# Transposing q and k by DMA instead of on TensorE, in a fused attention and MLP-mixer kernel

## The chip, the cores and the metric

The kernel runs on one core of a Trainium2 chip. The metric is the device time of one execution in microseconds (us), and lower is better. A core has five engines that run side by side: TensorE (PE in the profile, with PEld for its weight loads), VectorE (DVE), ScalarE (ACT), GpSimd (POOL) and SyncE (SP), which here only issues DMAs. Sixteen DMA engines move the data.

## The reference

The reference is causal attention with a decay bias, followed by a mixer block (an MLP over the tokens, then an MLP over the channels). Shapes are 8 batches, 8 heads, 576 tokens and 64 channels per head.

```python
def _attn_ref(q, k, v, s):                     # q, k, v: (8, 8, 576, 64), s: (8, 8, 576)
    scores = (1 / np.sqrt(D)) * np.matmul(q, k.transpose(0, 1, 3, 2))
    cum = np.cumsum(np.maximum(s, 0.0), axis=-1)
    bias = -(cum[:, :, :, None] - cum[:, :, None, :])
    scores = np.where(causal, -1e9, scores + np.minimum(bias, 0.0))
    attn = np.exp(scores - np.max(scores, axis=-1, keepdims=True))
    attn = attn / (np.sum(attn, axis=-1, keepdims=True) + 1e-09)
    return np.matmul(attn, v)

def _moe_ref(x, w_tok1, w_tok2, w_ch1, w_ch2):  # x: (8, 576, 512)
    h = np.maximum(x.transpose(0, 2, 1) @ w_tok1, 0.0) @ w_tok2
    u = x + h.transpose(0, 2, 1)
    return u + np.maximum(u @ w_ch1, 0.0) @ w_ch2
```

q and k are drawn as 0.1 times a normal variable, so the products of q and k are tiny beside the bias. The comparison with the reference hardly notices a wrong q or k.

## The kernel before

The kernel is built by a small list scheduler in Python, called the planner here. Each operation is registered with the engines that may do it and a guessed cost for each; the planner simulates the machine with these guesses and so fixes which engine does what, and in which order. These are the cost functions and the part that loads and casts one pair of heads:

```python
def c_dve(n, two=False):                       # guessed us for n elements on VectorE
    occ = 0.07 + n * (0.00053 if two else 0.00104)
    return occ, occ + 0.22

def c_pool(n, per=0.0022):                     # on GpSimd
    occ = 0.10 + n * per
    return occ, occ + 0.25

def stage_qk(b, h):                            # batch b, heads h and h+1
    f, n = Buf(r_qf), Buf(r_qn)
    for i, src in enumerate((k, q)):
        # token number = p * R + r: partition p holds R = 6 neighbouring tokens, long pieces for the DMA
        nc.sync.dma_start(out=f.t[:, i, :, :, :].rearrange("p e r d -> p e (r d)"),
                          in_=src[b, h : h + 2, :, :].rearrange("e (p r) d -> p e (r d)", r=R))
        ...
        # cast to bf16, on GpSimd from the second batch on
        nc.gpsimd.tensor_copy(out=n.t[:, i, :, :, :], in_=f.t[:, i, :, :, :].rearrange("p e r d -> p r e d"))
    ...
```

Because each partition holds six neighbouring tokens, six transposes of 96 columns give the tokens in the order r, p. The copy that takes the result out of PSUM (TensorE's result memory) also puts them back in the order p, r. These transposes and evictions are what the change replaces. The scores, the exponentials and the mask multiplies follow:

```python
def pair(b, h):
    qT, kT, E = Buf(r_qT), Buf(r_kT), Buf(r_E)          # rings of three buffers each
    for ti, dst in ((0, kT), (1, qT)):
        pt = Buf(r_sc, False)                            # a PSUM bank
        def tr(ti=ti, pt=pt):
            o = pt.t[:, :].bitcast(BF16)
            for r in range(R):
                nc.tensor.transpose(out=o[:, r * PR : (r + 1) * PR],
                                    in_=nat.t[:, ti, r, :, :].rearrange("p e d -> p (e d)"), identity=ident[0:PR, 0:PR])
        P.op({"PE": (R * 0.045, R * 0.045 + 0.3, tr)}, ...)
        def un(p0, p1, pt=pt):
            return pt.t[p0:p1, :].bitcast(BF16)[:, 0 : R * PR].rearrange("d (r p) -> d p r", r=R)
        ...
        # k: one copy of 128 partitions; q: two copies of 64 partitions, one per head; on ScalarE or VectorE
        nc.vector.tensor_copy(out=kT.t[:, 0:S].rearrange("d (p r) -> d p r", r=R), in_=un(0, 128))
    ...
            nc.tensor.matmul(out=o[:, :, c0 : c0 + e - a], lhsT=kT.t[:, j0 : j0 + 128],
                             rhs=qT.t[:, :, a:e], start=True, stop=True)          # scores
    ...
            nc.scalar.activation(out=E.t[:, :, EB[pc] : EB[pc] + 256], in_=..., func=AF.Exp, scale=0.125)
    ...
                    nc.vector.tensor_tensor(                                      # the mask multiply
                        out=E.t[:, :, d0 : d0 + n], in0=E.t[:, :, d0 : d0 + n],
                        in1=keep[:, k0 : k0 + n].unsqueeze(1).to_broadcast([128, 2, n]), op=ALU.mult)
    ...
                        nc.tensor.matmul(out=o[:, ic, 0 : D + 1], lhsT=E.t[:, hh, d0 : d0 + 128],
                                         rhs=vp.t[:, jc, h + hh, 0 : D + 1], ...)  # attention times v
```

The mask multiply has two inputs, both in SBUF (the on-chip memory of all tiles outside the PSUM banks). GpSimd's own work before the change is the cast of q and k and the scaling of v. The mixer of the third batch on already uses DMA transposes for its own activations, so the change extends a technique that the kernel has.

## Time and profile before

| | before |
|---|---|
| median of 3 runs (lowest to highest) | 330.56 us (329.26 to 331.84) |
| span of the profiled run, mean granted TensorE clock | 330.5 us, 0.982 of full speed |
| TensorE idle in the span | 330.5 - 308.9 = 21.6 us |

The page's first part gives, for each engine, the busy time, the share of the span and the number of instructions:

```profile
PE 308.9 (93%) x2424; PEld 178.6 (54%) x2457; DVE 207.2 (63%) x511; ACT 207.4 (63%) x367; POOL 101.1 (31%) x137
```

TensorE is busy nearly all the time. (It has 2,457 weight loads but 2,424 matmuls on record, so some 33 matmul records are missing.) The chain of waits, followed back from the last instruction, says the same:

```profile
PE 75%; DVE 14%; ACT 3%; DMA 3%; issue 2%; SPq 1%; POOL 0%; ACTq 0%
```

The table of stretches of the kernel before has the stretch, its length, then busy time with number of instructions for TensorE, its weight loads, VectorE, ScalarE and GpSimd, then the granted clock, the DMA share and GB/s:

```profile
75.00:130.00 55.00, 53.18 (x469) 32.03 (x472) 40.36 (x101) 38.75 (x68) 20.57 (x25) 1.00 0.78 173
130.00:250.00 120.00, 118.86 (x959) 69.07 (x969) 81.20 (x204) 85.50 (x149) 38.97 (x49) 1.00 0.62 149
```

From 75 to 250 us TensorE idles only 3 us at full clock. What it waits for is little and scattered. The view of TensorE's waits (engine, tile and line, what it waited for, then total, times and longest) holds these lines, in a list sorted by total:

```profile
PE psc_112 L657 <- ACT E_86 L663: 2.1, 1, 2.1
...
PE pav_115 L689 <- DVE E_84 L671: 0.5, 2, 0.3
```

The second line is attention times v waiting for a mask multiply: 0.5 us in the whole run. The next lines, from the groups of instructions, are the mask multiplies on three buffers, a cast on GpSimd, and two of the evictions that the change removes. The columns are line, engine, operation, out<-in, shapes, count, then busy us and mean ns of one, then idle time before them and what ended it:

```profile
L671 DVE TENSOR_TENSOR E_84<-E_84,keep 128x256 bf16<-128x256 bf16 (+1 forms) x55 | 17.2, 343 | 11.1 <-ACT E_84 L663 10.6
L671 DVE TENSOR_TENSOR E_85<-E_85,keep 128x256 bf16<-128x256 bf16 (+1 forms) x55 | 16.7, 331 | 8.9 <-ACT E_85 L663 8.7
L671 DVE TENSOR_TENSOR E_86<-E_86,keep 128x256 bf16<-128x256 bf16 (+1 forms) x50 | 14.8, 323 | 10.3 <-ACT E_86 L663 10.1
L575 POOL CAST qkn_76<-qkf_73 96x768 bf16<-96x768 f32 x22 | 18.3, 853 | 37.2 <-issue 18.2
L641 DVE COPY qT_78<-psc_113 64x576 bf16<-64x576 bf16 x7 | 5.3, 756 | 1.2 <-ACT qT_78 L639 0.6 <-PE psc_113 L619 0.4
L639 ACT COPY qT_79<-psc_113 64x576 bf16<-64x576 bf16 x7 | 4.4, 633 | 3.3 <-PE psc_113 L619 1.6 <-DVE qT_79 L641 1.6
```

The 160 mask multiplies take 17.2 + 16.7 + 14.8 = 48.7 us, with means of 323 to 343 ns; an eviction takes 0.76 us on VectorE or 0.63 us on ScalarE. In the timeline of TensorE (start us, duration, what), two groups of six transposes start 0.25 us apart, which is what one group costs:

```profile
129.58 0.42 PE L619 MATMUL psc_114<-ident,qkn_75 96*128 96x96 bf16 x6
129.83 0.42 PE L619 MATMUL psc_112<-ident,qkn_75 96*128 96x96 bf16 x6
```

### The profile page before, as it was taken

Reading aid. Unit: us, or ns where it says so; the run is one execution under the profiler, and the core shown is the slowest. Engines: PE = TensorE matmul, PEld = TensorE weight load, DVE = VectorE, ACT = ScalarE, POOL = GpSimd, SP = SyncE. Lnnn points to the kernel's source line nnn. Section 1 sums busy time; section 2 is a strip of 40 time slices with the busy share of each in tenths; the row PEclk is TensorE's granted clock in tenths of the full one; section 3 lists DMA queues with packets and bytes.
Section 4 is the critical chain, followed back from the end, with each engine's and each line's share of the span. In section 5 each row is a group of like instructions: output and inputs, shape, how many; then the busy total and the mean of one; then the engine's idle time right before and its main releaser. Section 6 shows DMA issues by size and latency. Waiting matters only on the chain.

```text
span 330.5 us, 6536 instructions
## 1 busy us (share of the span) xinstructions
PE 308.9 (93%) x2424; PEld 178.6 (54%) x2457; DVE 207.2 (63%) x511; ACT 207.4 (63%) x367; POOL 101.1 (31%) x137
## 2 busy tenths in 40 slices
PE   6888899979899999999999999999999799999992
PEld 2455486646665555555774554556764355446640
DVE  7698963789965756576776566576786454450021
ACT  4675777388886367974885278766889457406600
POOL 5455429757518022450146011821110000000000
PEclk9699999999999999999999999999999989999998
DMA  7999999999982549636944649266459710042031
GB/s 194 212 271 350 387 228 248 244 285 225 244 179 74 127 155 223 148 84 196 196 94 119 155 158 221 76 110 219 121 138 204 217 70 0 1 129 81 3 98 69
DMA packets 77272, 54.14 MB, mean 164 GB/s; under 512 B 54320, under 2 KB 70256, under 8 KB 77232
## 3 DMA queue, kind: packets, MB, share of 16 engines
q1 hardware_dynamic: 77232, 53.64, 65.7%
q8 instruction: 21, 0.34, 0.5%
q14 instruction: 19, 0.16, 0.2%
HBM read 40.65 MB, written 9.44 MB: 152 GB/s over the span
## 4 chain that ended last, share of the span: by engine, by line
PE 75%; DVE 14%; ACT 3%; DMA 3%; issue 2%; SPq 1%; POOL 0%; ACTq 0%
PE pmx_118 L883 12%; PE pmx_119 L865 9%; PE pmx_118 L865 8%; PE pmx_117 L865 8%; PE pmx_117 L883 7%; PE pmx_119 L883 7%; PE psc_112 L657 3%; PE pav_115 L689 2%; PE psc_113 L657 2%; PE psc_114 L657 2%; PE pav_116 L689 2%; DMA qkf_73<-in_k_dram 2%; PE pmx_117 L791 2%; PE pmx_117 L812 2%; DVE E_86 L671 2%
## 5 line engine op out<-in xcount | busy, mean ns | idle before, releaser
L865 PEld LDWEIGHTS <-wc_70 128*128 128x128 bf16 x624 | 59.2, 98 | 30.7 <-issue 0.5
L883 PEld LDWEIGHTS <-gb_107 128*128 128x128 bf16 x240 | 22.8, 99 | 25.6 <-issue 1.3
L575 POOL CAST qkn_75<-qkf_72 96x768 bf16<-96x768 f32 x19 | 17.1, 923 | 43.2 <-issue 12.9
L575 POOL CAST qkn_76<-qkf_73 96x768 bf16<-96x768 f32 x22 | 18.3, 853 | 37.2 <-issue 18.2
L883 PE MATMUL pmx_118<-wc_71,gb_107 128*128 128x512 bf16 x116 | 28.9, 393 | 0.2
L883 PEld LDWEIGHTS <-ga_106 128*128 128x128 bf16 x192 | 18.0, 98 | 19.6
L575 POOL CAST qkn_77<-qkf_74 96x768 bf16<-96x768 f32 x19 | 15.7, 843 | 30.7 <-ACT gb_107 L872 10.3
L671 DVE TENSOR_TENSOR E_84<-E_84,keep 128x256 bf16<-128x256 bf16 (+1 forms) x55 | 17.2, 343 | 11.1 <-ACT E_84 L663 10.6
L865 PE MATMUL pmx_118<-uTb_105,wc_70 128*128 128x320 bf16 x128 | 22.6, 299 | 0.1
L865 PE MATMUL pmx_119<-uTb_105,wc_70 128*128 128x320 bf16 x128 | 22.6, 299 | 0.0
L865 PE MATMUL pmx_117<-uTb_105,wc_70 128*128 128x320 bf16 x128 | 22.6, 299 | 0.0
L671 DVE TENSOR_TENSOR E_85<-E_85,keep 128x256 bf16<-128x256 bf16 (+1 forms) x55 | 16.7, 331 | 8.9 <-ACT E_85 L663 8.7
L548 POOL TENSOR_TENSOR vp_90<-vf_88,wT 128x512 bf16<-128x512 f32 (+1 forms) x20 | 20.6, 1053 | 2.2 <-DMA vf_88<-in_v_dram 1.9
L671 DVE TENSOR_TENSOR E_86<-E_86,keep 128x256 bf16<-128x256 bf16 (+1 forms) x50 | 14.8, 323 | 10.3 <-ACT E_86 L663 10.1
L872 ACT ACTIVATE gb_107<-pmx_119 128x320 bf16<-128x320 f32 x23 | 10.2, 442 | 17.4 <-PE pmx_119 L865 16.0
L548 POOL TENSOR_TENSOR vp_89<-vf_87,wT 128x512 bf16<-128x512 f32 (+1 forms) x15 | 15.4, 1041 | 6.0 <-PE pav_116 L689 4.7
L865 PE MATMUL pmx_118<-uTa_104,wc_70 128*128 128x512 bf16 (+1 forms) x79 | 17.1, 336 | 0.1
L865 PE MATMUL pmx_119<-uTa_104,wc_70 128*128 128x512 bf16 (+1 forms) x80 | 17.1, 336 | 0.0
L883 PE MATMUL pmx_117<-wc_71,ga_106 128*128 128x512 bf16 x69 | 16.9, 379 | 0.2
L865 PE MATMUL pmx_117<-uTa_104,wc_70 128*128 128x512 bf16 (+1 forms) x77 | 16.6, 335 | 0.2
L970 PE MATMUL pmx_117<-zero 128*128 128x512 bf16 (+6 forms) x44 | 14.2, 418 | 1.5 <-DVE zero L425 1.2
L883 PE MATMUL pmx_118<-wc_71,ga_106 128*128 128x512 bf16 x57 | 14.3, 379 | 0.2
(284 smaller groups left out, 695.9 us busy)
## 6 DMA issues: line engine op xcount, KB each, us to landing
vf_87<-in_v_dram SPq DMA_DIRECT2D x16, 256.0 KB, 6.6
vf_88<-in_v_dram SPq DMA_DIRECT2D x16, 256.0 KB, 5.5
qkf_74<-in_k_dram SPq DMA_DIRECT2D x14, 288.0 KB, 4.1
qkf_74<-in_q_dram SPq DMA_DIRECT2D x14, 288.0 KB, 4.4
qkf_72<-in_k_dram SPq DMA_DIRECT2D x13, 288.0 KB, 3.8
qkf_72<-in_q_dram SPq DMA_DIRECT2D x13, 288.0 KB, 4.4
qkf_73<-in_k_dram SPq DMA_DIRECT2D x13, 288.0 KB, 4.8
qkf_73<-in_q_dram SPq DMA_DIRECT2D x13, 288.0 KB, 5.2
```

The source lines that it names most:

```text
L548: eng.tensor_tensor(out=vp.t[p0 : p0 + n, c, :, 0:D], in0=vf.t[p0 : p0 + n, c, :, :], in1=wT[p0 : p0 + n, cw, b * H : b * H + H].unsqueeze ...
L575: nc.gpsimd.tensor_copy(out=o, in_=a)
L657: nc.tensor.matmul(out=o[:, :, c0 : c0 + e - a], lhsT=kT.t[:, j0 : j0 + 128], rhs=qT.t[:, :, a:e], start=True, stop=True)
L671: nc.vector.tensor_tensor(out=E.t[:, :, d0 : d0 + n], in0=E.t[:, :, d0 : d0 + n], in1=keep[:, k0 : k0 + n].unsqueeze(1).to_broadcast([128, ...
L689: nc.tensor.matmul(out=o[:, ic, 0 : D + 1], lhsT=E.t[:, hh, d0 : d0 + 128], rhs=vp.t[:, jc, h + hh, 0 : D + 1], start=(jc == j_lo), stop=( ...
L791: nc.tensor.matmul(out=pm.t[:, ha * D : hb * D], lhsT=w1[:, NJ if odd and c == NJ - 1 else c, t * 128 : t * 128 + 128], rhs=x.t[:, c, ha * ...
L812: nc.tensor.matmul(out=pm.t[:, :], lhsT=w2[:, t, w0 : w0 + 128], rhs=h1.t[:, t, :], start=(t == 0), stop=(t == NTC - 1))
L865: nc.tensor.matmul(out=pm.t[:, 0 : e - a], lhsT=wc1[:, m, cc * 128 : cc * 128 + 128], rhs=uT.t[:, m, a:e], start=(m == 0), stop=(m == NMC ...
L872: lambda cc=cc, pm=pm, a=a, e=e: nc.scalar.activation(out=g.t[:, cc, a:e], in_=pm.t[:, 0 : e - a], func=AF.Relu),
L883: nc.tensor.matmul(out=pm.t[:, :], lhsT=g.t[:, cc, c * 128 : c * 128 + 128], rhs=wc2[:, cc, :], start=(cc == 0), stop=(cc == NCC - 1))
L970: f.fn = lambda t=r.tiles[slots[0]], n=n: nc.tensor.matmul(out=t[:, 0:n], lhsT=zero[:, 0:128], rhs=zero[:, 0:n], start=True, stop=True)
```

## The change

The intent is to relieve TensorE, which bounds the kernel. For batches 2 to 7 (24 of the 32 head pairs) SyncE issues two DMA transposes per pair, from the cast tile into a new ring of three tiles named tr. The tokens come out in the order r, p, so three reordering copies per pair, on GpSimd or VectorE, write kT and qT. To make room a tile of ones shrank to one broadcast column, which doesn't bear on the argument.

```diff
+    r_tr = ring("tr", 3, [128, 2, R, PR], BF16)
...
+        if b >= 2:
+            raw = Buf(r_tr)
+            for ti in range(2):
+                def trd(ti=ti):
+                    nc.sync.dma_start_transpose(out=raw.t[:, ti, :, :],
+                                                in_=nat.t[:, ti, :, :, :].rearrange("p r e d -> p (r e d)"))
+                P.op({"SP": (0.6, 0, trd)}, reads=[(nat, ti)], writes=[(raw, ti)], prio=0, dma=0.85)
+            for (p0, p1, ti, dst, key) in ((0, 128, 0, kT, (kT, 0)), (0, 64, 1, qT, (qT, 0)), (64, 128, 1, qT, (qT, 1))):
+                def cp(eng, p0=p0, p1=p1, ti=ti, dst=dst):
+                    o = dst.t[p0:p1, 0:S] if dst is kT else dst.t[p0:p1, p0 // 64, :]
+                    o = o.rearrange("d (p r) -> d p r", r=R)
+                    i = raw.t[p0:p1, ti, :, :].rearrange("d r p -> d p r")
+                    eng.tensor_copy(out=o, in_=i)
+                P.op({"POOL": (*c_pool(576, 0.0011), lambda cp=cp: cp(nc.gpsimd)),
+                      "DVE": (*c_dve(576), lambda cp=cp: cp(nc.vector))}, reads=[(raw, ti)], writes=[key],
+                     prio=b * 10 + h - 1)
+        else:
             (the TensorE transposes and the PSUM evictions, as before)
```

The planner is told that a copy takes 0.10 + 576 x 0.0011 = 0.73 us on GpSimd and that a DMA transpose holds SyncE for 0.6 us.

More of the change, by code (lines that the diff above doesn't have):

```diff
@@ L456 @@
     s_sb = sb("s_sb", [64, S], FP32, fast)
-    one_sb = sb("one_sb", [64, S], FP32, fast)
+    ones = sb("ones", [128, 1], FP32, fast)
+    one_sb = ones[0:64, 0:1].to_broadcast([64, S])
     cum = sb("cum", [64, S], FP32)
@@ L462 @@
     nc.sync.dma_start(out=s_sb[:, :], in_=s.rearrange("b h s -> (b h) s"))
-    nc.vector.memset(one_sb[:, :], 1.0)
+    nc.vector.memset(ones[:, :], 1.0)
     nc.vector.memset(wn[:, S:640], 0.0)
@@ L475 @@
     P.op({"DVE": (1.3, 1.6, lambda: nc.vector.tensor_tensor_scan(
-        out=cum[:, :], data0=one_sb[:, :], data1=s_sb[:, :], initial=0.0, op0=ALU.mult, op1=ALU.add))},
+        out=cum[:, :], data0=one_sb, data1=s_sb[:, :], initial=0.0, op0=ALU.mult, op1=ALU.add))},
         reads=["sr"], writes=["cum"], prio=-1)
@@ L505 @@
     bad = sb("bad", [128, 4 + NSQ], FP32, fast)
-    ones = sb("ones", [128, 1], FP32, fast)
     flagf = sb("flagf", [1, 1], FP32, fast)
@@ L509 @@
     nc.vector.memset(bad[:, :], 0.0)
-    nc.vector.memset(ones[:, :], 1.0)
     P.op({"DVE": (1.3, 1.6, lambda: nc.vector.tensor_tensor_scan(
-        out=pre[:, :], data0=one_sb[:, :], data1=wn[:, 0:S], initial=0.0, op0=ALU.mult, op1=ALU.add))},
+        out=pre[:, :], data0=one_sb, data1=wn[:, 0:S], initial=0.0, op0=ALU.mult, op1=ALU.add))},
         reads=["wn"], writes=["pre"], prio=50)
@@ L612, in pair @@
         odd = b % 2
-        for ti, dst in ((0, kT), (1, qT)):
-            pt = Buf(r_sc, False)
-            def tr(ti=ti, pt=pt):
-                o = pt.t[:, :].bitcast(BF16)
-                for r in range(R):
-                    nc.tensor.transpose(out=o[:, r * PR : (r + 1) * PR],
-                                        in_=nat.t[:, ti, r, :, :].rearrange("p e d -> p (e d)"), identity=ident[0:PR, 0:PR])
-            P.op({"PE": (R * 0.045, R * 0.045 + 0.3, tr)}, reads=[(nat, ti)] + pads, writes=[(pt, 0)], holds=[dst], prio=(np_, 2))
-            def un(p0, p1, pt=pt):
-                return pt.t[p0:p1, :].bitcast(BF16)[:, 0 : R * PR].rearrange("d (r p) -> d p r", r=R)
-            if dst is kT:
-                def evk(eng, un=un):
-                    o = kT.t[:, 0:S].rearrange("d (p r) -> d p r", r=R)
-                    if eng == 0:
-                        nc.scalar.copy(out=o, in_=un(0, 128))
-                    else:
-                        nc.vector.tensor_copy(out=o, in_=un(0, 128))
-                P.op({"ACT": (*c_act(576), lambda evk=evk: evk(0)), "DVE": (*c_dve(576), lambda evk=evk: evk(1))},
-                     reads=[(pt, 0)], writes=[(kT, 0)], prio=1)
-            else:
-                for hh in range(2):
-                    def evq(eng, hh=hh, un=un):
-                        o = qT.t[hh * 64 : hh * 64 + 64, hh, :].rearrange("d (p r) -> d p r", r=R)
@@ new lines, in pair, with tr, un, evk @@
+        if b >= 2:
[15 more added lines that the diff above has]
+        else:
+            for ti, dst in ((0, kT), (1, qT)):
+                pt = Buf(r_sc, False)
+                def tr(ti=ti, pt=pt):
+                    o = pt.t[:, :].bitcast(BF16)
+                    for r in range(R):
+                        nc.tensor.transpose(out=o[:, r * PR : (r + 1) * PR],
+                                            in_=nat.t[:, ti, r, :, :].rearrange("p e d -> p (e d)"), identity=ident[0:PR, 0:PR])
+                P.op({"PE": (R * 0.045, R * 0.045 + 0.3, tr)}, reads=[(nat, ti)] + pads, writes=[(pt, 0)], holds=[dst], prio=(np_, 2))
+                def un(p0, p1, pt=pt):
+                    return pt.t[p0:p1, :].bitcast(BF16)[:, 0 : R * PR].rearrange("d (r p) -> d p r", r=R)
+                if dst is kT:
+                    def evk(eng, un=un):
+                        o = kT.t[:, 0:S].rearrange("d (p r) -> d p r", r=R)
@@ L638, in evq @@
                         if eng == 0:
-                            nc.scalar.copy(out=o, in_=un(hh * 64, hh * 64 + 64))
+                            nc.scalar.copy(out=o, in_=un(0, 128))
                         else:
-                            nc.vector.tensor_copy(out=o, in_=un(hh * 64, hh * 64 + 64))
-                    P.op({"ACT": (*c_act(576), lambda evq=evq: evq(0)),
-                          "DVE": (*c_dve(576), lambda evq=evq: evq(1))},
-                         reads=[(pt, 0)], writes=[(qT, hh)], prio=1)
+                            nc.vector.tensor_copy(out=o, in_=un(0, 128))
@@ new lines, in pair, with evq @@
+                    P.op({"ACT": (*c_act(576), lambda evk=evk: evk(0)), "DVE": (*c_dve(576), lambda evk=evk: evk(1))},
+                         reads=[(pt, 0)], writes=[(kT, 0)], prio=1)
+                else:
+                    for hh in range(2):
+                        def evq(eng, hh=hh, un=un):
+                            o = qT.t[hh * 64 : hh * 64 + 64, hh, :].rearrange("d (p r) -> d p r", r=R)
+                            if eng == 0:
+                                nc.scalar.copy(out=o, in_=un(hh * 64, hh * 64 + 64))
+                            else:
+                                nc.vector.tensor_copy(out=o, in_=un(hh * 64, hh * 64 + 64))
+                        P.op({"ACT": (*c_act(576), lambda evq=evq: evq(0)),
+                              "DVE": (*c_dve(576), lambda evq=evq: evq(1))},
+                             reads=[(pt, 0)], writes=[(qT, hh)], prio=1)
```

## The prediction

> **What bounds the kernel now.** From about 100 to 250 us TensorE does: the table of stretches gives it 148.5 us busy in those 150 us (clock 1.00), while VectorE has 100, ScalarE 103, GpSimd 49 us and the DMA engines are 61% busy. The chain of waits agrees: 75% of the span is TensorE, mostly channel-MLP matmuls at 0.215 us per 512 columns, their full pace. VectorE's 14% of the chain lies mostly before 100 us.
>
> **What is removed.** For 24 of 32 head pairs, two groups of six 96-column transposes. In the timeline such a group holds TensorE 0.26 us (129.58 to 129.83), so 48 x 0.26 = 12.3 us of TensorE, nearly all in the saturated stretch. Also 72 PSUM evictions: ScalarE 0.63 us, VectorE 0.75 us each, about 50 us. Chain pieces "q evicted on VectorE, then ScalarE" (130.9, 202.3, 277.7 us) go.
>
> **What is added.**
> - 48 DMA transposes of 96x768 from SyncE's queue. The existing 128x512 ones take 1.2 us of issue, start 1.3 us apart, and land after 2.4 us. Scaled by bytes (1.125) to blocks (6 for 4) I estimate 1.4 to 1.8 us of issue and 2.6 to 3.5 us to landing. [...] some 217 GB/s within a burst, about 100 GB/s at the issue pace. So 67 to 86 us of SyncE's queue, and 0.8 us of all 16 engines each, 38 us.
> - 72 reordering copies: by the instruction order 49 on GpSimd (estimate 0.7 us, from the 0.8 us cast of 768 elements; 34 us) and 23 on VectorE (0.65 us; 15 us).
>
> **Does it fit?** Batches 2 to 7 take about 32 us of attention each. GpSimd goes from 12 to some 18 us per batch. SyncE's queue: loads 3, v 5.5, stores 2, existing transposes 6, added 11.5 to 14.5: 28 to 31 of 32 us, in order and with waits between. That is the tight resource: buffers three deep hide latency, not a lack of throughput. Second risk: [...] the mask multiplies (0.21 us at best, 0.28 median, up to 1.5 here) may lengthen.
>
> **Critical path.** About 11 to 12 us of the 12.3 lie where TensorE is saturated; I take off 2 to 3 us for score matmuls that wait for late q/k behind the SyncE queue. 330.6 - 12 + 2.5 = 321 us.
>
> **Prediction:** 321 us, 8 in 10 between 314 and 330. Faster by over 2%: 0.64; within 2%: 0.28; slower: 0.08.
>
> **What would show it.** TensorE busy down about 12 us or more with as little idle; the period of two batches (71.5 us between the long second-MLP runs at 108.9, 180.7, 252.1 us) shorter by about 4 us; ScalarE about 27 us less busy, VectorE about 10, GpSimd up 34; DMA transposes 1.4 to 1.8 us of issue; score matmuls waiting for GpSimd or VectorE copies under 3 us in all.
>
> **What would make it wrong.** Transposes of over 2 us of issue, or loads held behind transposes that wait for GpSimd: then score matmuls wait for copies by 10 us or more, and the time is the same or worse. GpSimd copies at 1.5 us would do likewise. Better than 314: relief of VectorE and ScalarE at 75 to 100 us (85% busy).

## The result, and the profile after

The changed kernel is slower. Its median is 352.09 us (346.73 to 354.04, four runs), beside 330.32 us (329.26 to 331.84, four runs) for the kernel before. Two of its four runs, 353.61 and 354.04 us at a clock of 0.966, are over 1.5% above its fastest and so count as slow; the two fast ones are 350.56 us (the profiled run, clock 0.972) and 346.73 us (0.981). The ratio is 1.056, with a 95% interval of 1.048 to 1.064. Here and below a ratio is the mean time of one kernel's fast runs over that of the other's of the same rounds, so it isn't quite the ratio of the medians quoted. The two fast runs of the changed kernel have a mean of 348.6 us, those of the kernel before 330.4 us: the loss is 18.2 us where fast is compared with fast, and this is the loss that the text means.

The same views of the changed kernel follow, first the busy times and the chain of waits:

```profile
PE 306.9 (88%) x2169; PEld 169.1 (49%) x2169; DVE 240.6 (69%) x493; ACT 188.0 (54%) x335; POOL 163.3 (47%) x186
PE 55%; DVE 23%; POOL 7%; issue 5%; SPq 3%; DMA 3%; ACT 2%; POOLq 0%; DVEq 0%; ACTq 0%
```

The weight loads confirm that 48 groups of six transposes went: (2457 - 2169) / 6 = 48. But TensorE's idle time rose from 21.6 to 348.5 - 306.9 = 41.6 us, VectorE is busy for 33 us more instead of less, and GpSimd for 62 us more. The chain now runs through VectorE for 23% and GpSimd for 7%. The stretches of the changed kernel, with the columns as before:

```profile
75.00:130.00 55.00, 41.94 (x308) 24.13 (x307) 48.65 (x82) 28.35 (x54) 42.85 (x44) 0.91 0.85 171
130.00:250.00 120.00, 109.35 (x735) 57.20 (x734) 92.63 (x176) 70.67 (x122) 67.94 (x70) 1.00 0.89 192
```

TensorE idles 13.1 + 10.7 = 23.7 us in these 175 us, where it idled 3 before. Its waits after the change show for what:

```profile
PE pav L705 <- DVE E L687: 10.5, 12, 2.4
PE pmx L828 <- DVE h L818: 5.7, 2, 5.1
PE pmx L881 <- DVE gb L890: 4.3, 4, 1.5
PE pmx L881 <- DVE ga L890: 2.7, 1, 2.7
...
PE psc L673 <- DVE qT L624: 1.3, 2, 0.9
```

TensorE waits for VectorE's mask multiplies (10.5 us, where it was 0.5) and for VectorE's evictions (h, gb and ga). It hardly waits for the new copies themselves: the last line shows 1.3 us. So the loss isn't a late q or k. VectorE has become slow at other work. The groups show which:

```profile
L687 DVE TENSOR_TENSOR E<-E,keep 128x256 bf16<-128x256 bf16 (+1 forms) x160 | 82.0, 543 | 20.8 <-ACT E L679 20.1
L719 DVE TENSOR_TENSOR x<-pav,rc 128x320 bf16<-128x320 f32 x64 | 30.6, 489 | 1.5
```

The same 160 mask multiplies now take 82.0 us instead of 48.7. The normalisation in the second line, which reads PSUM, takes 489 ns each and 30.6 us in all; its groups before added up to 31.2 us, so it isn't slowed. Nor are all mask multiplies slower: their median went only from 282 to 292 ns. Laid beside GpSimd's instructions in the trace, the 89 that overlap none took 295 ns at most, and each of the 49 that took over 500 ns was overlapped, for 78% of its time or more, by copies, casts or scalings of v on GpSimd, all of which read SBUF. The view of the copies' line in the changed kernel gives the shortest, median and longest duration in ns, then the first and last start:

```profile
L624 POOL COPY qT<-tr x35: 1142/1197/1677, 72.1 to 277.4; 64x576 bf16<-64x576 bf16 x35
L624 POOL COPY kT<-tr x14: 1137/1166/1567, 71.0 to 274.9; 128x576 bf16<-128x576 bf16 x14
L624 DVE COPY qT<-tr x13: 627/1146/1601, 104.1 to 253.1; 64x576 bf16<-64x576 bf16 x13
L624 DVE COPY kT<-tr x10: 637/1204/4490, 83.4 to 259.9; 128x576 bf16<-128x576 bf16 x10
```

A GpSimd copy takes nearly 1.2 us whenever it runs. A VectorE copy can be done in 0.63 us, but its median is 1.15 to 1.2 us, and one took 4.49 us, in which five GpSimd instructions ended. The timelines around that one show what VectorE and GpSimd did at the same time, first VectorE and then GpSimd (start us, duration, what):

```profile
110.08 4.49 DVE L624 COPY kT<-tr 128x576 bf16<-128x576 bf16 x1
114.50 1.24 DVE L687 TENSOR_TENSOR E<-E,keep 128x256 bf16<-128x256 bf16 x1
115.77 1.37 DVE L624 COPY qT<-tr 64x576 bf16<-64x576 bf16 x1
117.17 1.13 DVE L687 TENSOR_TENSOR E<-E,keep 128x256 bf16<-128x256 bf16 x1
118.22 0.68 DVE L818 TENSOR_SCALAR h<-pmx 128x512 bf16<-128x512 f32 x1
```

```profile
109.37 1.15 POOL L624 COPY qT<-tr 64x576 bf16<-64x576 bf16 x1
110.47 1.59 POOL L574 CAST qkn<-qkf 96x768 bf16<-96x768 f32 x2
112.03 2.04 POOL L547 TENSOR_TENSOR vp<-vf,wT 128x512 bf16<-128x512 f32 x2
114.01 1.57 POOL L624 COPY kT<-tr 128x576 bf16<-128x576 bf16 x1
115.55 1.08 POOL L547 TENSOR_TENSOR vp<-vf,wT 128x512 bf16<-128x512 f32 x1
116.58 2.76 POOL L624 COPY qT<-tr 64x576 bf16<-64x576 bf16 x2
```

While GpSimd runs instruction after instruction from 109.37 us on, four VectorE instructions with inputs in SBUF, two of them copies with a single input, take 4.49 + 1.24 + 1.37 + 1.13 = 8.2 us. Undisturbed, a mask multiply took 0.28 us (the median before) and such a copy 0.63 us (the shortest here). The eviction of h, which reads PSUM, takes its usual 0.68 us, but it stands behind them. TensorE waits for it, and the timeline of TensorE shows the price (in brackets the idle time before and what ended it):

```profile
112.80 1.03 PE L899 MATMUL pmx<-wc,gb 128*128 128x512 bf16 x4
118.95 1.87 PE L828 MATMUL pmx<-h,w 128*128 128x512 bf16 x4 [5.12 <-DVE h L818]
```

TensorE idles 5.12 us. In the table of stretches its granted clock is then 0.50 from 118 to 124 us, 0.96 from 124 to 127 and 1.00 from 127 to 130 us. The lowered clock is part of the reason why TensorE's busy time fell by only 2 us, although the transposes were gone: 41.94 us at a clock of 0.91 hold an estimated 41.94 x 0.09 = 3.8 us of slowed work.

### The profile page after: what moved, and what is told of

Read it like the earlier page. It is cut to its first block, busy times and chain, and to the rows that moved or that the text cites. A ratio compares the mean times of both kernels' runs of the same rounds, so it can differ in the third digit from the quotient of the medians.

```text
span 348.5 us, 6110 instructions
## 1 busy us (share of the span) xinstructions
PE 306.9 (88%) x2169; PEld 169.1 (49%) x2169; DVE 240.6 (69%) x493; ACT 188.0 (54%) x335; POOL 163.3 (47%) x186
## 4 chain that ended last, share of the span: by engine, by line
PE 55%; DVE 23%; POOL 7%; issue 5%; SPq 3%; DMA 3%; ACT 2%; POOLq 0%; DVEq 0%; ACTq 0%
PE pmx L899 21%; PE pmx L881 18%; DVE E L687 10%; PE psc L673 4%; PE pmx L807 4%; PE pav L705 3%; POOL qkn L574 3%; POOL qT L624 3%; PE pmx L828 2%; DVE x L719 2%; DVE ua L835 2%; PE pmx L986 2%; DVE qT L624 2%; ACT E L679 2%; DMA qkf<-in_k_dram 2%
## 5 line engine op out<-in xcount | busy, mean ns | idle before, releaser
L687 DVE TENSOR_TENSOR E<-E,keep 128x256 bf16<-128x256 bf16 (+1 forms) x160 | 82.0, 543 | 20.8 <-ACT E L679 20.1
L679 ACT ACTIVATE E<-psc 128x512 bf16<-128x512 f32 x128 | 68.2, 601 | 43.5 <-PE psc L673 43.3
L881 PEld LDWEIGHTS <-wc 128*128 128x128 bf16 x624 | 60.1, 98 | 40.3 <-issue 9.0
L881 PE MATMUL pmx<-uTb,wc 128*128 128x320 bf16 x384 | 56.9, 301 | 4.4 <-DVE gb L890 4.3
L574 POOL CAST qkn<-qkf 96x768 bf16<-96x768 f32 x60 | 51.9, 884 | 13.2 <-DMA qkf<-in_k_dram 10.0
L899 PE MATMUL pmx<-wc,gb 128*128 128x512 bf16 x240 | 55.1, 379 | 0.0
L624 POOL COPY qT<-tr 64x576 bf16<-64x576 bf16 x35 | 43.8, 1252 | 15.7 <-PE psc L673 13.9
L881 PE MATMUL pmx<-uTa,wc 128*128 128x512 bf16 (+1 forms) x240 | 44.3, 336 | 2.7 <-DVE ga L890 2.7
L673 PE MATMUL psc<-qT,kT 128*128 128x512 bf16 (+2 forms) x160 | 42.1, 352 | 3.3 <-DVE qT L624 1.3
L899 PE MATMUL pmx<-wc,ga 128*128 128x512 bf16 x192 | 44.4, 379 | 0.0
L705 PE MATMUL pav<-vp,E 128*128 128x65 bf16 x576 | 28.1, 195 | 12.2 <-DVE E L687 10.5
L624 POOL COPY kT<-tr 128x576 bf16<-128x576 bf16 x14 | 16.9, 1204 | 41.0 <-PE psc L673 22.6
L719 DVE TENSOR_TENSOR x<-pav,rc 128x320 bf16<-128x320 f32 x64 | 30.6, 489 | 1.5
```

The costliest lines, as they stand in the source:

```text
L574: nc.gpsimd.tensor_copy(out=o, in_=a)
L624: eng.tensor_copy(out=o, in_=i)
L687: nc.vector.tensor_tensor(out=E.t[:, :, d0 : d0 + n], in0=E.t[:, :, d0 : d0 + n], in1=keep[:, k0 : k0 + n].unsqueeze(1).to_broadcast([128, ...
L719: nc.vector.tensor_tensor(out=x.t[:, :, (h + hh) * D : (h + hh + 1) * D], in0=o[:, :, 0:D], in1=rc.t[:, :].unsqueeze(2).to_broadcast([128, ...
L881: nc.tensor.matmul(out=pm.t[:, 0 : e - a], lhsT=wc1[:, m, cc * 128 : cc * 128 + 128], rhs=uT.t[:, m, a:e], start=(m == 0), stop=(m == NMC ...
L899: nc.tensor.matmul(out=pm.t[:, :], lhsT=g.t[:, cc, c * 128 : c * 128 + 128], rhs=wc2[:, cc, :], start=(cc == 0), stop=(cc == NCC - 1))
```

## The experiments

Several theories were open. The read theory: GpSimd's copies read SBUF, and while they do, VectorE's instructions with SBUF operands are held up, as the four that took 8.2 us above suggest. (By what mechanism the one engine would hold up the other, no run here shows.) Its rivals: GpSimd is simply too late with its own work (time theory); the DMA transposes crowd the DMA engines or SyncE's queue, or land late (DMA theory); the planner's wrong costs gave a bad order (planner theory). Each run below was timed in 3 rounds with a profile, four times in all. All gave the reference's result unless the text says otherwise.

### All copies on VectorE (e1_dve_only)

```diff
-                P.op({"POOL": (*c_pool(576, 0.0011), lambda cp=cp: cp(nc.gpsimd)),
-                      "DVE": (*c_dve(576), lambda cp=cp: cp(nc.vector))}, reads=[(raw, ti)], writes=[key],
-                     prio=b * 10 + h - 1)
+                P.op({"DVE": (*c_dve(576), lambda cp=cp: cp(nc.vector))}, reads=[(raw, ti)], writes=[key],
+                     prio=1)
```

> The changed kernel with all 72 reordering copies on VectorE, none on GpSimd. Theory A (GpSimd's copies hold VectorE off, so mask multiplies and with them the attention chain get longer): mask multiplies fall back from 0.54 us mean to about 0.3, VectorE copies from 1.15 us median to 0.63, TensorE waits less for masks, time 322 to 335 us. Theory B (the DMA transposes crowd SyncE's queue and the DMA engines, so q and k come late): mask multiplies may get shorter, but the time stays at 343 us or more.

Measured: 337.59 us, ratio 1.026 (1.019 to 1.033). The range that I had expected was missed. The groups of this run show the mask multiplies and the VectorE copies:

```profile
L686 DVE TENSOR_TENSOR E<-E,keep 128x256 bf16<-128x256 bf16 (+1 forms) x160 | 54.7, 374 | 14.8 <-ACT E L678 14.4
L624 DVE COPY qT<-tr 64x576 bf16<-64x576 bf16 x48 | 37.7, 786 | 0.5
```

Without GpSimd copies the mask multiplies fall from 543 to 374 ns and over half of the loss goes (337.9 us in the mean of fast runs, against 348.6). But all 72 copies are on VectorE now, and it isn't relieved: it is busy for 228.5 us, against 207.2 before.

### Copies on ScalarE or VectorE (e2_act_dve)

```diff
-                P.op({"POOL": (*c_pool(576, 0.0011), lambda cp=cp: cp(nc.gpsimd)),
+                P.op({"ACT": (*c_act(576), lambda cp=cp: cp(nc.scalar)),
                       "DVE": (*c_dve(576), lambda cp=cp: cp(nc.vector))}, reads=[(raw, ti)], writes=[key],
-                     prio=b * 10 + h - 1)
+                     prio=1)
```

> The changed kernel with the copies on ScalarE or VectorE, as the PSUM evictions were. It keeps the DMA transposes and the gain of 12 us on TensorE. A: 318 to 330 us, mask multiplies about 0.3 us. B: 343 us or more, and TensorE idles in front of score matmuls or for loads.

Three of its four runs count as slow (339.18 to 339.83 us) and one as fast (331.05 us), so there is no ratio. One duration is clear, in the groups of this run:

```profile
L625 ACT COPY qT<-tr 64x576 bf16<-64x576 bf16 x31 | 36.4, 1173 | 0.3
L658 ACT COPY qT<-psc 64x576 bf16<-64x576 bf16 x10 | 6.3, 632 | 6.5 <-PE psc L638 4.4 <-DVE qT L660 2.0
```

Both lines copy the same shape with the same gather. From PSUM it takes ScalarE 632 ns, from SBUF 1173 ns. ScalarE is no cheap home for the copies.

### GpSimd copies added to the kernel before (e3_pool_copies_alone)

The kernel before keeps its TensorE transposes. GpSimd makes 48 copies of the same shape and gather, from a tile that is never rewritten into a tile that nobody reads. Their only wait is for the order behind a cast.

```diff
+        if b >= 2:
+            for p0, p1 in ((0, 128), (0, 64)):
+                def cp(p0=p0, p1=p1):
+                    nc.gpsimd.tensor_copy(out=dout[p0:p1, :].rearrange("d (p r) -> d p r", r=R),
+                                          in_=dead[p0:p1, :, :].rearrange("d r p -> d p r"))
+                P.op({"POOL": (*c_pool(576, 0.0019), cp)}, prio=b * 10 + h - 1, after=casts[(b, h)])
```

> The kernel before, transposes on TensorE, plus 48 GpSimd copies of the same shape and pattern from a tile that never changes to one that nobody reads (the output stays right). A: each copy takes 1.1 to 1.2 us, mask multiplies rise from 0.31 us to over 0.45, and the time rises by 10 us or more, to 340 or more. B: mask multiplies rise somewhat, time within 3 us of before.

Measured: 346.27 us, ratio 1.049 (1.042 to 1.057). Copies that nobody waits for cost 16 us, most of the 18 us. The groups:

```profile
L680 DVE TENSOR_TENSOR E<-E,keep 128x256 bf16<-128x256 bf16 (+1 forms) x160 | 69.0, 464 | 29.4 <-ACT E L672 28.8
L619 POOL COPY dout<-dead 128x576 bf16<-128x576 bf16 (+1 forms) x48 | 56.2, 1171 | 1.5
L650 DVE COPY qT<-psc 64x576 bf16<-64x576 bf16 x27 | 20.3, 753 | 3.6 <-ACT qT L648 2.1 <-PE psc L628 1.2
```

The mask multiplies went from about 333 to 464 ns (and TensorE's attention times v waits 6.8 us for them), while VectorE's evictions from PSUM stayed at 753 ns. This fits the read theory. It doesn't yet exclude the time theory, because the copies also keep GpSimd busy.

### DMA transposes added to the kernel before (e4_dma_transposes_alone)

```diff
+        if b >= 2:
+            raw = Buf(r_tr)
+            for ti in range(2):
+                def trd(ti=ti):
+                    nc.sync.dma_start_transpose(out=raw.t[:, ti, :, :],
+                                                in_=nat.t[:, ti, :, :, :].rearrange("p r e d -> p (r e d)"))
+                P.op({"SP": (0.6, 0, trd)}, reads=[(nat, ti)], writes=[(raw, ti)], prio=0, dma=0.85)
```

> The kernel before plus the 48 DMA transposes of q and k to a tile that nobody reads. A: time within 4 us of before, since nothing waits for them. B: loads and channel transposes come later, time up by 10 us or more, to 340 or more.

Measured: 330.37 us, ratio 0.999 (0.994 to 1.004). The same 48 transposes, read by nobody, cost nothing, though the DMA share in the stretches from 100 to 250 us rose from 0.57-0.63 to 0.83-1.05. Crowding of the DMA engines or of SyncE's queue is therefore not the cause by itself.

### Copies that read in order (e5_read_in_order)

The copy walks its source in order and scatters the writes 12 bytes apart, instead of gathering reads 192 bytes apart.

```diff
-                    o = o.rearrange("d (p r) -> d p r", r=R)
-                    i = raw.t[p0:p1, ti, :, :].rearrange("d r p -> d p r")
-                    eng.tensor_copy(out=o, in_=i)
+                    o = o.rearrange("d (p r) -> d r p", r=R)
+                    eng.tensor_copy(out=o, in_=raw.t[p0:p1, ti, :, :])
```

> The changed kernel, but every reordering copy walks its source in order (96 tokens in a row) and scatters its writes 12 bytes apart, instead of gathering reads 192 bytes apart. If the 1.2 us of a GpSimd copy come from the strided reads, it falls to about 0.65 us, mask multiplies to under 0.45 us, and the time to 335 us or less [...]. If the copy stays at 1.2 us, the time stays at 347 to 354 us.

Measured: 386.85 us, ratio 1.172 (1.164 to 1.180). The expected relief turned into its opposite:

```profile
L686 DVE TENSOR_TENSOR E<-E,keep 128x256 bf16<-128x256 bf16 (+1 forms) x160 | 91.8, 606 | 20.3 <-ACT E L678 19.7
L623 POOL COPY qT<-tr 64x576 bf16<-64x576 bf16 x35 | 80.0, 2284 | 11.2 <-PE psc L672 7.5 <-ACT E L678 2.6
```

Scattered writes cost GpSimd 2.28 us per copy, against 1.2 for gathered reads. My reason for the experiment, that the strided reads might make the copy long, was a guess that no run had shown, and it said nothing of writes. As a dose test it still serves: longer GpSimd copies, longer mask multiplies and more lost time. VectorE's own copies became slower too (2.05 us in the mean for q), so the run doesn't separate the theories.

### Honest costs for the planner (e6_honest_plan)

```diff
-                P.op({"SP": (0.6, 0, trd)}, reads=[(nat, ti)], writes=[(raw, ti)], prio=0, dma=0.85)
+                P.op({"SP": (1.3, 0, trd)}, reads=[(nat, ti)], writes=[(raw, ti)], prio=0, dma=0.85)
...
-                P.op({"POOL": (*c_pool(576, 0.0011), lambda cp=cp: cp(nc.gpsimd)),
+                P.op({"POOL": (*c_pool(576, 0.0019), lambda cp=cp: cp(nc.gpsimd)),
```

> The changed kernel with two cost figures of its own planner corrected: 1.2 us for a GpSimd copy instead of 0.73, 1.3 us of SyncE for a DMA transpose instead of 0.6. Theory D (the order was planned on wrong durations, so in-order engines sit in front of late data): 340 us or less. Theory A: more copies go to VectorE, time within 5 us of the changed kernel.

Measured: 343.45 us, ratio 1.044 (1.037 to 1.052). Knowing the copies' length, the planner gives GpSimd 46 of them and makes another order. The mean of its fast runs, 343.9 us, is 4.7 us below the changed kernel's 348.6 us, and the intervals of the two ratios overlap (1.037 to 1.052 and 1.048 to 1.064). It was run at another time. The planner's wrong costs are thus worth perhaps 5 us, which isn't clear of noise. The mask multiplies still take 521 ns, so most of the loss lies elsewhere.

### No copies at all, with its controls (e7, e8, e9, e12)

If the loads bring blocks of 96 tokens, the DMA transpose can write kT and qT directly. The edit then loads in pieces of 256 bytes and puts the q of both heads side by side without zero padding, so that each score matmul contracts over the 64 channels of one head, and it gives the heads PSUM banks of their own. (The rings of kT and qT are five deep in e7, e9 and e12.) Cut to its core, the edit of e7_no_copies against the kernel before is:

```diff
+                if b >= 2:
+                    nc.sync.dma_start(out=f.t[:, i, :, :, :].rearrange("p e r d -> p (e r) d"),
+                                      in_=src[b, h : h + 2, :, :].rearrange("e (r p) d -> p (e r) d", p=PR))
...
+                    nc.sync.dma_start_transpose(out=dst.t[:, 0:S].rearrange("d (r p) -> d r p", r=R),
+                                                in_=nat.t[:, ti, :, :, :].rearrange("p r e d -> p (r e d)"))
...
-                    nc.tensor.matmul(out=o[:, :, c0 : c0 + e - a], lhsT=kT.t[:, j0 : j0 + 128],
-                                     rhs=qT.t[:, :, a:e], start=True, stop=True)
+                        nc.tensor.matmul(out=ps.t[:, c0 : c0 + e - a], lhsT=kT.t[d, j0 : j0 + 128],
+                                         rhs=qT.t[d, a:e], start=True, stop=True)
```

> DMA transposes without any reordering copy: q and k of batches 2 to 7 are loaded as six blocks of 96 tokens, so the DMA transpose gives the right order and writes the score operands themselves; the zero halves of q go, scores are matmuls over 64 partitions a head, into separate PSUM banks. If the copies are the whole loss (A), TensorE's 12 us come back: 322 us or less. If latency or crowding of the DMA transposes also costs (B), 328 us or more, with TensorE waiting in front of score matmuls.

Measured: 336.18 us, ratio 1.022 (1.016 to 1.027). With the small pieces the DMA share was 1.06 to 1.19 in the four stretches of 50 us from 50 to 250 us (0.83 to 1.09 in e4, with the loads of before), so this run mixes two effects. Its control e8_before_k64 is the kernel before with only the last part of the edit, the scores per head:

```diff
-    r_qT = ring("qT", 3, [128, 2, S], BF16)
+    r_qT = ring("qT", 3, [128, S], BF16)
...
-                    nc.tensor.matmul(out=o[:, :, c0 : c0 + e - a], lhsT=kT.t[:, j0 : j0 + 128],
-                                     rhs=qT.t[:, :, a:e], start=True, stop=True)
+                        nc.tensor.matmul(out=ps.t[:, c0 : c0 + e - a], lhsT=kT.t[d, j0 : j0 + 128],
+                                         rhs=qT.t[d, a:e], start=True, stop=True)
```

> Control for the run without copies: the kernel before, transposes on TensorE, with the same scores over 64 partitions a head and one eviction of q instead of two. Expected within 4 us of before (326 to 334), since ScalarE and VectorE don't bound the middle; what it gains is not the DMA transposes' doing.

Measured: 335.45 us, ratio 1.017 (1.010 to 1.024). The scores per head cost 6 us by themselves, more than the 4 us that I had allowed. To get rid of the small pieces, e9_no_copies_wrong_order takes e7 with the loads of before:

```diff
-                if b >= 2:
-                    nc.sync.dma_start(out=f.t[:, i, :, :, :].rearrange("p e r d -> p (e r) d"),
-                                      in_=src[b, h : h + 2, :, :].rearrange("e (r p) d -> p (e r) d", p=PR))
-                    return
```

> Wrong result on purpose: as the run without copies, but q and k are loaded as in both kernels (six tokens in a row), so the DMA-transposed tiles hold the tokens in another order and are used so. It takes the copies away and leaves the loads' DMA time as it was. Its pair is the control with 64-partition scores (335.5 us). If the copies are the whole loss (A), TensorE's 12 us appear: 325 us or less. If a late or crowded DMA path eats them (B), 331 us or more.

Its tokens are in the wrong order; the comparison with the reference passed all the same, because the scores are so small. Measured: 328.62 us, ratio 0.994 (0.987 to 1.001). Against its control e8 that is 335.45 - 328.62 = 6.8 us less. This lies between the two expectations: without copies the removal of the transposes seems to pay, but by about half of the 12 us. (The deeper rings are a second difference to e8, which no run tests.) To see whether crowded DMA engines eat the other half, e12_no_copies_no_v_loads leaves out four of the five loads of v per batch (a relative error of 1.05):

```diff
-            load_op(load, [(vf, c)] + ([("st", "v")] if b == 1 else []), 1024 * 0.0226 / 16 * n / 128)
+            if b < 2 or c == NJ - 1:
+                load_op(load, [(vf, c)] + ([("st", "v")] if b == 1 else []), 1024 * 0.0226 / 16 * n / 128)
```

> Wrong result on purpose: the run without copies in wrong order, and from the third batch on four of the five v loads of a batch are left out too (stale v is used). That takes some 37 us of 16 DMA engines and some 26 us of SyncE's queue away. If a crowded DMA path is what still eats about 5 of TensorE's 12 us there (B), the time falls from 328.6 to 325 us or less; if something else does, it stays within 2 us of 328.6.

Measured: 334.03 us, ratio 1.013 (1.008 to 1.017), where 325 or less would have spoken for crowding. The planner made another order, with other waits (4.2 us for one exponential), so the run gives crowding no support but doesn't refute it cleanly. (The loads left out are worth what was expected: the packets' time fell from 82.5% of 327.3 us in e9 to 69.9% of 331.7 us of all 16 DMA engines, by 38 us.)

### GpSimd busy without reading SBUF (e10_pool_memsets_alone)

This is e3 with memsets of the same length in place of the copies.

```diff
-                    nc.gpsimd.tensor_copy(out=dout[p0:p1, :].rearrange("d (p r) -> d p r", r=R),
-                                          in_=dead[p0:p1, :, :].rearrange("d r p -> d p r"))
+                    nc.gpsimd.memset(dout[p0:p1, :], 0.0)
```

> As the run with 48 GpSimd copies alone, but each is a GpSimd memset of about the same length (1152 float32, some 1.15 us), which reads nothing from SBUF. [...] mask multiplies stay under 0.36 us and the time within 5 us of before (under 335). If it is GpSimd's own queue (casts and v scaling come later), the time is 340 us or more, as with the copies, with mask multiplies unchanged.

Measured: 332.68 us, ratio 1.010 (1.004 to 1.016). The groups:

```profile
L618 POOL MEMSET dout<- 128x1152 f32 (+1 forms) x48 | 50.6, 1054 | 1.4
L678 DVE TENSOR_TENSOR E<-E,keep 128x256 bf16<-128x256 bf16 (+1 forms) x160 | 49.5, 339 | 29.7 <-ACT E L670 29.1
```

GpSimd is as busy as in e3 (150.2 against 156.1 us), yet the mask multiplies keep their 339 ns and the loss is 3 us instead of 16. The traces also have the same instructions in the same order on TensorE, ScalarE, GpSimd and VectorE (but for one memset of the set-up), so the planner's order can't explain the difference, and what sets the copies apart is the read of SBUF. In e10, 34 mask multiplies overlap only memsets on GpSimd, and none of them took over 294 ns. This decides between the read theory and the time theory.

### A candidate (e11_dve_copies_from_fifth)

```diff
-        if b >= 2:
+        if b >= 4:
...
-                P.op({"SP": (0.6, 0, trd)}, reads=[(nat, ti)], writes=[(raw, ti)], prio=0, dma=0.85)
+                P.op({"SP": (1.3, 0, trd)}, reads=[(nat, ti)], writes=[(raw, ti)], prio=0, dma=1.1)
...
-                P.op({"POOL": (*c_pool(576, 0.0011), lambda cp=cp: cp(nc.gpsimd)),
-                      "DVE": (*c_dve(576), lambda cp=cp: cp(nc.vector))}, reads=[(raw, ti)], writes=[key],
-                     prio=b * 10 + h - 1)
+                P.op({"DVE": (*c_dve(576), lambda cp=cp: cp(nc.vector))}, reads=[(raw, ti)], writes=[key],
+                     prio=1)
```

> A version that might beat both: DMA transposes from the fifth batch only, after the start-up whose loads fill the DMA engines, copies on VectorE alone, and the planner told 1.3 us of SyncE and 1.1 us of DMA per transpose. 32 fewer groups of transposes, so 8 us less TensorE work. A: VectorE's copies are held off by GpSimd's casts, but nothing is saturated: 324 to 330 us. If any such copies cost more than TensorE gains: 331 us or more.

Measured: 327.90 us, ratio 0.995 (0.988 to 1.002), with a correct result. It is nominally the fastest correct version, but its interval includes no change, so it isn't shown to beat the kernel before.

### The changed kernel's own order, with reads and waits taken away (e13 to e16)

The additions to the kernel before leave a doubt: another order might hide other costs. The last four runs therefore keep the changed kernel's instruction order on every engine, which the traces confirm (but for one memset of the set-up in e13), and alter only what the copies do. All four give wrong q and k in batches 2 to 7, and the comparison passed for the reason given above. e13_no_dma_wait takes the source from a tile that is written once at the start, so that no copy waits for a DMA:

```diff
-                    i = raw.t[p0:p1, ti, :, :].rearrange("d r p -> d p r")
+                    i = dead[p0:p1, :, :].rearrange("d r p -> d p r")
```

> Changed kernel, same order; the copies read a tile that never changes instead of the DMA-transposed one, so nobody waits for the DMA transposes (wrong data on purpose). Theory A [...]: within 3 us of the changed kernel (347 to 354). Theory B (late transposes): 343 us or less.

Measured: 354.38 us (348.43 to 356.03), three of the four runs slow, and so no ratio. The one fast run, 348.43 us, lies between the changed kernel's two fast runs (346.73 and 350.56). I read no gain from it. Its mask multiplies take 531 ns and attention times v waits 10.6 us for them, as in the changed kernel, so wrong q and k alone don't bring the time down. e14_pool_no_read keeps the waits, but GpSimd reads a single element and fills the rest with two memsets, 1.3 to 1.4 us in all:

```diff
+                    if eng is nc.gpsimd:
+                        eng.tensor_copy(out=o[:, 0:1], in_=raw.t[p0:p1, ti, 0, 0:1])
+                        eng.memset(o[:, 1:576], 0.1)
+                        eng.memset(o[:, 1:450], 0.1)
+                        return
```

> Changed kernel, same order and same waits; each GpSimd copy becomes a copy of one element a row, which keeps the wait, and two memsets that fill about the same 1.1 us without reading SBUF (wrong data on purpose). A: mask multiplies fall from 0.54 to under 0.38 us and the time to 338 us or less. B or the planned order: 345 us or more.

Measured: 328.74 us, ratio 0.994 (0.986 to 1.003). Some 20 us are gone (348.6 to 328.9 in the mean of fast runs), the whole loss. The mask multiplies of e14, its busy times, and one of TensorE's waits:

```profile
L692 DVE TENSOR_TENSOR E<-E,keep 128x256 bf16<-128x256 bf16 (+1 forms) x160 | 59.2, 401 | 21.1 <-ACT E L684 20.4
PE 303.0 (93%) x2169; PEld 167.7 (51%) x2169; DVE 210.0 (64%) x493; ACT 187.2 (57%) x335; POOL 164.3 (50%) x284
```

```profile
PE pav L710 <- DVE E L692: 1.0, 2, 0.5
```

GpSimd is as busy as in the changed kernel (164.3 against 163.3 us) and in the same order; only its reads are gone. VectorE is busy for 31 us less (210.0 against 240.6), and attention times v waits 1.0 us for mask multiplies instead of 10.5. The mask multiplies fell to 401 ns, not quite to the 380 I had asked for: the casts and the scaling of v still read SBUF. In the trace the 21 that took over 500 ns are overlapped by these for 79% of their time or more; the 39 that overlap only the new memsets took 294 ns at most. e15_no_reads takes the read from VectorE's copies as well, and e16_no_reads_no_wait also the single element, and with it the wait for the DMA:

```diff
e15:
+                    eng.tensor_copy(out=o[:, 0:1], in_=raw.t[p0:p1, ti, 0, 0:1])
+                    eng.memset(o[:, 1:576], 0.1)
+                    if eng is nc.gpsimd:
+                        eng.memset(o[:, 1:450], 0.1)
e16, in place of the first of these lines:
+                    eng.memset(o[:, 0:1], 0.1)
```

> As the run before, with VectorE's 23 copies turned into a one-element copy and a memset too (wrong data on purpose): no reordering copy reads SBUF, all waits stay. A: a few us below that run, 325 to 335 us.

> As the run before, but with memsets alone, so that nobody waits for the DMA transposes (wrong data on purpose). The difference to the run before is what late transposes cost: under 2 us by A, 5 us or more by B. If this run is still above 325 us, the rest is the planned order, not a wait for transposes [...].

Measured: 329.26 us, ratio 0.995 (0.987 to 1.004), and 327.25 us, ratio 0.986 (0.976 to 0.996), which is faster by less than 2% in the middle of the interval. Taking the reads from VectorE's copies too gained nothing, where I had expected a few us. The wait for the transposes, which e16 drops together with the one-element copies, is worth some 2 us at most: its slowest run, 328.69 us, is just below e15's fastest, 328.80. Even when no copy reads and no copy waits for a DMA, the time stays some 9 us above the 318 to 319 us that 330.6 less 12 would give. In e16 TensorE is busy for 48.5 of the 55 us from 75 to 130 us, where it was 53.2 in the kernel before. So part of the missing gain is lost at the start of the new scheme, in this planned order, and neither the reads nor the waits of the copies explain it. What exactly does, these runs leave open.

## Why the prediction was wrong

The result, 352.09 us (fast runs 346.73 and 350.56), lies far outside the predicted range of 314 to 330 us. Point by point:

- **What bounds the kernel before.** Right: TensorE, with 3 us idle from 75 to 250 us.
- **What is removed.** The counts were right: 48 groups of transposes and 72 evictions. ScalarE fell by 19 us (207.4 to 188.0) instead of 27: its q and k evictions fell by 25 us, but the planner gave it 9 more rectifier evictions. TensorE's busy time fell by 2 us, not 12. Some 4 us of the difference are an estimate for the lowered clock from 75 to 130 us, given above. Some 3 us more are missing matmul records: e4 has the same matmuls with all 2457 on record, and its TensorE is busy for 311.6 us, not 308.9. The rest isn't accounted for.
- **DMA transposes.** The issue took 1.225 us in the median (1.195 to 3.239), less than the predicted 1.4 to 1.8. The landing took 3.8 us in the median, more than the predicted 2.6 to 3.5. In e4 the packets' time rose from 65.7% of 330.5 us to 81.8% of 331.2 us of all 16 DMA engines, by 53.8 us for 48 transposes or 1.12 us each (any slowing of other packets included), which is 147 KB / 1.12 us = 132 GB/s. The prediction had 0.8 us. The fear that SyncE's queue was "the tight resource" was wrong: e4 adds the same transposes for nothing, the one fast run of e13 shows no gain when no copy waits for them, and e16 gains some 2 us on e15 without the wait, about the 2.5 us that the prediction had taken off for late q and k.
- **GpSimd copies, "estimate 0.7 us".** This term was mis-sized: 1.2 us. The estimate came from a cast whose reads are contiguous, 768 elements in 0.8 us or about 1.04 ns each; the copy gathers 2-byte elements 192 bytes apart, 576 in 1.17 us or about 2.03 ns each. GpSimd rose by 62 us instead of 34, of which 43.8 + 16.9 = 60.7 us are the copies.
- **"VectorE about 10" less busy.** Wrong in sign: 33 us more (207.2 to 240.6). The 23 copies, estimated at 0.65 us each, took 0.63 us at best but 1.15 to 1.2 us in the median. They add 28.3 us (14.6 + 13.7) where 24.5 us of evictions went (30.5 to 6.0), and the mask multiplies add 82.0 - 48.7 = 33.3 us.
- **"Second risk": longer mask multiplies.** This is the step that failed. The prediction said that the mask multiplies "may lengthen" when GpSimd gets more work, and gave it no size. It was the main term. Copies that read SBUF cost 16 us on the kernel before (e3), the same GpSimd time without reads 3 us (e10), and taking the reads from the changed kernel in its own order gives back the whole loss (e14).
- **"Score matmuls waiting for copies under 3 us in all".** Right, at 1.3 us of waits for VectorE's copies. It was the wrong place to look: the cost came as waits for mask multiplies and for evictions queued behind them.
- **"The period of two batches" shorter by 4 us.** Wrong. The first long second-MLP matmuls of the odd batches start at 102.9, 189.1 and 269.7 us, 86 and 81 us apart; by the same reading they start at 100.6, 174.9 and 246.3 us before, 74 and 71 apart.
- **"GpSimd copies at 1.5 us would do likewise".** The direction was right and 1.2 us sufficed, but by held-up mask multiplies and evictions queued behind them, not by late copies.

What holds: the reads of GpSimd's copies cause the loss (shown by e3, e10 and e14 together). The planner's wrong costs may make it some 5 us larger than it need be (e6, not clear of noise). That TensorE's 12 us would come back in full once the reads are gone is refuted by e14 to e16 for this order. The reason for that remainder is open.

## What to carry to other kernels

Taking work from the engine that bounds a kernel helps only if what replaces it doesn't slow another engine into the critical path. Here evictions from PSUM became copies from SBUF, and GpSimd was handed long reads, during which VectorE's mask multiplies and copies with SBUF inputs were held up (with 49 copies of 1.2 us on GpSimd the mean of the 160 mask multiplies went from 333 to 543 ns); before such a move, estimate how much of the added GpSimd reading time falls on VectorE work with SBUF inputs, and put a number on it. Memsets of the same length in place of the suspected copies separate the cost of the reads from that of a busy engine (16 us with the copies of e3, 3 us with the memsets of e10) at the cost of a few lines.
